# Packed attention and a gated feed-forward on one core: another order of the first batch's loads, and twelve products ahead of TensorE's order

## The chip, the core and the metric

The kernel runs on one core of a Trainium2 chip. TensorE (PE in the rows) multiplies matrices and transposes through a product with an identity matrix, VectorE (DVE), ScalarE (ACT) and GpSimd (POOL) work on elements, and SyncE (SP) issues transfers between the chip's memory and the core's own. ScalarE can issue transfers too. The metric is the time of one execution in microseconds (us), from the first to the last instruction of the core with the little that lies around it. Of the kernel before there are three timed runs, 739.72 to 740.54 us, median 739.77 us.

## The reference

```python
# batch 8, heads H = 8, seq S = 576, D = 64; p has 32 rows for each head
def sm_attn(qq, kk, vv):
    s = scale * np.matmul(qq, kk.transpose(0, 1, 3, 2))
    s = s - np.max(s, axis=-1, keepdims=True)
    a = np.exp(s)
    a = a / (np.sum(a, axis=-1, keepdims=True) + 1e-09)
    return np.matmul(a, vv)

p_packed = sm_attn(p, k, v)              # stage 1: 32 queries for each head
out = sm_attn(q, p_packed, p_packed)     # stage 2: 576 queries on 32 keys
x = out.transpose(0, 2, 1, 3).reshape(4608, 512)
result = (x @ w_a) * (x @ w_b) @ w_out   # w_a, w_b: 512 x 1536, w_out: 1536 x 512
```

All inputs and the output are float32.

## The kernel before

The kernel goes through the batch in eight steps of 576 tokens. For each it computes stage 1 of the attention (`stage1`, two groups of four heads), stage 2 (`stage2`, the same two groups) and then the feed-forward. The feed-forward has a trick: instead of forming x and multiplying it by w_a and w_b, `g_tiles` (L332) multiplies the 32 packed rows of each head with w_a and w_b first, and `mm1` (L351) multiplies the attention weights of stage 2 with that. The product of the two halves goes through `mm2_part` (L377) with w_out. The large operands are split in a high and a low part (`a_hi`, `a_lo`, `ghi`, `glo`), and three products make up one.

While TensorE does the feed-forward of one batch step, the attention of the next is woven in between its products. Only the first batch step has nothing to be woven into: its inputs have to be loaded, turned and sent through both attention stages before the first product of `mm1` can run. This stretch at the start is what the change touches.

The inputs of the first batch step are loaded by `load_first` (k and q, in three parts each: 0 and 1 are 512 rows of four heads each, 2 is the rest of all heads), `load_v` (two groups) and `load_p`. `turn_first` (L147, L152) turns k and q on TensorE, into a bank of PSUM, and VectorE (L149) or ScalarE (L149, L154) copies the result to `xT`. `turned` (L236) does so for p, and later for the result of stage 1 (`ppT`, L237). Stage 1's first products are L247, its softmax L253 to L261, its turned weights L271 to L274, its second products L281. Stage 2's first products are L297, and its softmax runs on VectorE, ScalarE and GpSimd, L302 to L319.

The weights w_a, w_b and w_out are stored as float32 words that have to be changed before use, in three steps per piece, which the orders call A (`high_word`, L189, ScalarE), B (`low_word`, L197 on ScalarE or L194 on VectorE or GpSimd) and C (`both_words`, L200, VectorE). Twelve buffers hold pieces (512 KB each); C frees one, and with it the next load can go.

Every engine does its instructions in the order in which they are written (`manual_schedule`), so four strings of names set the work of each engine: `FIRST` is the order of the first loads, `START` that of all steps up to the first `mm1`, `PLAN_0` and `PLAN` what is woven into the first batch step's feed-forward and the later ones'. In `FIRST` a name is an input and a part (p0, k0, k1, k2, q0 to q2, v0, v1; w1 loads one piece of a weight). In `START`, T turns p, k and q turn a part, S and r are the steps of stage 1, P turns its result, s are the steps of stage 2, A, B and C convert a piece, L loads for the next batch step, and g starts `g_tiles`. W is `warm` (L519): nine products of the identity with a tile of k, which nobody reads (L524, 128x512 each).

```python
    FIRST = ("p0 k0 k2 k1 q0 v0 q1 v1 q2 w1 w1 w1 w1 w1 w1 w1 w1 w1 w1 w1")
    START = ("T0 k0 k4 k1 k3 k2 q0 S0 S1 r0 r1 q1 r1 r0 r0 r1 r0 q2 r1 q3 q4 P0 s0 B s1 W A s0 B A A s0 s0 B s1 C "
```

Of the kernel before, what the change touches and what calls it, by code (L numbers as in the profile page):

```python
# [19 lines left out]
def tile_packed_attn_gated_ffn(  # L20
# [20 lines left out]
    nc = tc.nc  # L41
    B, H, S, D = q.shape
# [3 lines left out]
    P = 128  # L46
    R, E = 4, 2
# [6 lines left out]
    TR = HS - 2 * P  # L54
# [17 lines left out]
    ident = const.tile([P, P], F32, name="ident")  # L72
# [18 lines left out]
    def bank_pair(s=False):  # L91
        return ps_s.tile([P, 2, 512], F32, name="s") if s else ps_m.tile([P, 2, 512], F32, name="m")
# [9 lines left out]
    def load(src, key, b, i):  # L102


        t = ld.tile([P, R, XH, TL], F32, name=f"nat{i}")
        rows = src[b, R * i:R * i + R].rearrange("h s d -> (h s) d")
        rows = rows.rearrange("(y l u) d -> u l y d" if key == "k" else "(y u l) d -> u l y d", u=2, l=TL)
        for u in range(2):
            for w in range(2):
                g = 64 * u + 32 * w  # L110
                nc.sync.dma_start(
                    out=t[g:g + TL].rearrange("l h x d -> l (h x) d"), in_=rows[u][:, :, TL * w:TL * w + TL])
        nats[key, b, i] = t

    def turn(key, b, i):

        t = nats.pop((key, b, i))
        xT = ld.tile([P, R, HS], F32, name=f"xT{i}")
        nc.vector.transpose(out=xT.rearrange("p h t -> p (h t)"), in_=t.rearrange("p h x d -> p (h x d)"))  # L119
        xTs.setdefault((b, key), []).append(xT)  # L120
# [2 lines left out]

    firsts = {}

    def load_first(src, key, part):

        if part < 2:
            t = scratch.tile([P, R, 4 * D], F32, name=f"{key}n{part}")
            nc.sync.dma_start(  # L130
                out=t, in_=src[0, R * part:R * part + R, 0:4 * P, :].rearrange("h (p i) d -> p h (i d)", i=4))
        else:
            t = scratch.tile([P, H, 2 * D], F32, name=f"{key}n{part}")
            nc.sync.dma_start(out=t[0:TR], in_=src[0, :, 4 * P:S, :].rearrange("h (p u) d -> p h (u d)", u=2))
        firsts[key, part] = t

    def turn_first(key, n):
# [17 lines left out]

    vts, p_nat = {}, {}

    def load_v(b, e):


        t = ld.tile([P, R, NT, D], F32, name="vt") if b or e == 0 else scratch.tile([P, R, NT, D], F32, name="vt1")
        vv = v[b].rearrange("(r e) s d -> e s r d", e=E)[e]
        n = 2 if b else 4
        for i in range(4 // n):
            nc.sync.dma_start(
                out=t[:, :, n * i:n * i + n, :].rearrange("p r u d -> p r (u d)"),
                in_=vv[n * P * i:n * P * i + n * P].rearrange("(p u) r d -> p r u d", u=n).rearrange("p r u d -> p r (u d)"))
        for u in range(2):
            nc.sync.dma_start(
                out=t[TR * u:TR * u + TR, :, 4, :],  # L170
                in_=vv[4 * P:S].rearrange("(p u) r d -> u p r d", u=2)[u])
        vts[b, e] = t

    def load_p(b):
        t = sm.tile([P, E + 1, D], F32, name="p_nat", bufs=1)
        for e in range(E + 1):
            nc.sync.dma_start(out=t[:, e, :], in_=p[b].rearrange("(r e) j d -> e r j d", e=E)[e % E])  # L177
        p_nat[b] = t

    def xT_cols(b, key, u, h, cols=slice(0, HS)):  # L180
# [50 lines left out]
    def turned(dst, src, back=0):  # L231

        tp = bank()
        cols = src.rearrange("p e d -> p (e d)")
        for i in range(2):
            nc.tensor.transpose(tp[:, P * i:P * i + P], cols[:, 64 * (i ^ back):64 * (i ^ back) + P], ident)  # L236
        nc.vector.tensor_copy(out=dst.rearrange("p i r j -> p (i r j)"), in_=tp[:, 0:2 * P])  # L237
# [178 lines left out]
    def drain(g):  # L416
        for _ in g:
            pass

    def emit(b, plan, tasks={}):  # L420

        for name in plan.split():
            if name in tasks:
                next(tasks[name], None)
                continue
            if name == "W":
                warm()
                continue
            if name in "ABCD":
                convert(name)  # L430
                continue
            what, e = name[:-1], int(name[-1])
            n = b + (e // 2 if b or what[0] == "L" else 0)
            if n >= B:
                continue
            if what == "S":
                if e == 0:
                    st[b] = [stage1(b, 0), stage1(b, 1), stage2(b, 0), stage2(b, 1)]
                next(st[b][e])
            elif what == "s":  # L440
                next(st[b][2 + e], None)
            elif what == "r":
                next(st[b][e], None)
            elif what == "T":
                turned(pT, p_nat.pop(n))
            elif what == "P":
                turned(ppT[:, b % 2:b % 2 + 2], pp.pop(b), b % 2)
            elif what in ("k", "q"):
                turn(what, n, e % 2) if b else turn_first(what, e)
            elif what == "Lk":  # L450
                load(k, "k", n, e % 2)
            elif what == "Lq":
                load(q, "q", n, e % 2)
            elif what == "Lv":
                load_v(n, e % 2)
            elif what == "Lp":
                load_p(n)

    st = {}

    FIRST = ("p0 k0 k2 k1 q0 v0 q1 v1 q2 w1 w1 w1 w1 w1 w1 w1 w1 w1 w1 w1")
    START = ("T0 k0 k4 k1 k3 k2 q0 S0 S1 r0 r1 q1 r1 r0 r0 r1 r0 q2 r1 q3 q4 P0 s0 B s1 W A s0 B A A s0 s0 B s1 C "
             "A s1 B s0 C s1 A s1 C B B Lp2 C A B A s0 s1 B C B B s0 B g A C A A s1 Lv2 Lk2 C C A A C B B Lk3 C s1")
    WAYS = ("000000022220202120012012011200010010")
    TURN = ("0001110101")
    SUBS = ("0100")
# [1 line left out]
    PLAN = (" | S0 | r0 |  | r0 | r0 |  | r0 Lv1 |  | S1 | r1 | q0 Lk2 | r1 |  |  | r1 q1 Lk3 |  | r1 Lv2 |  |  | "  # L468
            "T2 P0 |  |  | s0 s0 s1 g s0 |  | s1 | Lp4 s0 s1 s1 k2 | s0 | s0 | s1 s0 | s1 Lq2 | s1 | k3 Lq3")
    PLAN = dict(enumerate(PLAN.split("|")))  # L470
    PLAN_0 = ("A | C C | B A B A | B C C B C | A A | C | B | C B A T0 k0 Lp2 A | A A B B C Lq0 | C C k1 | A B A | "
# [3 lines left out]
    PLAN_0 = dict(enumerate(PLAN_0.split("|")))  # L475

# [13 lines left out]
    def convert(x):  # L490

        if x == "D":
            if wo_f32:
                split_wout(wo_f32.pop(0))
                load_pieces(2)
            return
        if not to_do[x]:
            return
        c, n = to_do[x].pop(0)
        if (c, n) not in raws:  # L500
            load_pieces(1)
        raw = raws[c, n]
        if x == "A":
            high_word(raw)
        elif x == "B":
            low_word(raw, int(WAYS[pieces.index((c, n))]))
        else:
            assert len(to_do["A"]) <= len(to_do[x]) and len(to_do["B"]) <= len(to_do[x])
            if c < NC:
                i, rr = divmod(n, 2)  # L510
                both_words(w_ab[:, c, 2 * rr:2 * rr + 2, 2 * P * i:2 * P * i + 2 * P], raw)
            else:
                t = sm.tile([P, DO], F32, name="wo_f32", bufs=1)
                both_words(t, raw)
                wo_f32.append(t)
            del raws[c, n]
            load_pieces(2)

    def warm(n=9):  # L519

        x = bank_pair()[:, 0, :]
        t = firsts["k", 0].rearrange("p h t -> p (h t)")
        for _ in range(n):
            nc.tensor.matmul(out=x, lhsT=ident, rhs=t[:, 0:512], start=True, stop=True)  # L524

    def next_g(b):

        gnext[:] = g_tiles(b, 0)
        yield

    ET = mybir.EngineType
    ep(tc.manual_schedule(engines={ET.PE, ET.DVE, ET.Activation, ET.Pool, ET.SP}))
    for name in FIRST.split():
        what, i = name[0], int(name[1])
        if what == "p":
            load_p(0)
        elif what == "v":
            load_v(0, i)
        elif what == "w":
            load_pieces(i)  # L540
        else:
            load_first(k if what == "k" else q, what, i)
    gnext = []
    tasks = {"g": next_g(0)}
    emit(0, START, tasks)
    drain(tasks["g"])
    early.__exit__(None, None, None)
# [5 lines left out]
    for b in range(B):  # L553
        plan = dict(PLAN if b else PLAN_0)
        slot, tasks = [0], {"g": next_g(b + 1)}
# [73 lines left out]
```

## Time and profile before

| | us |
|---|---|
| median of three timed runs | 739.77 |
| the profiled execution, its own time | 739.7 |
| its span, first to last instruction | 737.9 |
| TensorE busy | 724.8 (98%) |
| first transfer of k issued | 2.74 |
| first transpose of k on TensorE | 7.29 |
| first product of stage 1 | 12.92 |
| first product of mm1 | 35.09 |

Times inside the profile are counted from the start of the span. The profiled execution's own time is 1.8 us longer than its span; that part lies around the span. A row of an engine's timeline gives start, length, engine, line, the written and read tiles, shapes and the number of instructions merged into it; ends of products are modelled, so the distance from one start to the next tells more than the length. In brackets stands how long the engine was idle before, and what ended that. TensorE's 98% leave some 13 us of the span in which no product is recorded, and nearly all of those lie before the first product of `mm1`.

### The profile page before, as it was taken

What the parts mean: (1) busy time and instruction counts of PE and PEld (TensorE: products, weight loads), DVE (VectorE), ACT (ScalarE), POOL (GpSimd) and SP (SyncE); (2) the same over time, 40 slices, a digit from 0 to 9 for tenths busy, and PEclk for the clock granted to TensorE, in tenths of its full rate; (3) what the DMA queues carried; (4) which work ended last, traced back from release to release, by engine and by line L of the source; (5) the groups of instructions that cost most, each with busy time, mean ns of one, the idle gap of its engine ahead of it and who ended that gap; (6) DMA issues with size and microseconds to landing.
All of it is one profiled execution on the core that took longest, in us unless ns stands there. A gap on an engine that the chain in (4) does not pass through costs nothing.

```text
span 737.9 us, 13756 instructions
## 1 busy us (share of the span) xinstructions
PE 724.8 (98%) x5862; PEld 606.0 (82%) x5862; DVE 302.4 (41%) x487; ACT 282.6 (38%) x495; POOL 212.5 (29%) x154
## 2 busy tenths in 40 slices
PE   6899999999999999999999999999999999999998
PEld 4488977888888888888888888888888888888887
DVE  2888655456114561344503545045610456023200
ACT  3788744553125531444204442144311543134300
POOL 0586752334003340234202341033400334023300
PEclk9999999999999999999999999999999999999999
DMA  8999945250501514033310333115050100000001
GB/s 251 379 260 297 257 88 99 57 97 17 97 30 33 98 30 84 16 66 70 74 48 16 65 71 77 47 33 97 5 104 30 34 1 17 28 15 2 1 29 43
DMA packets 171005, 58.30 MB, mean 79 GB/s; under 512 B 140608, under 2 KB 158784, under 8 KB 170944
## 3 DMA queue, kind: packets, MB, share of 16 engines
q1 hardware_dynamic: 170944, 57.43, 31.9%
q8 instruction: 46, 0.75, 0.4%
q14 instruction: 15, 0.12, 0.1%
HBM read 47.97 MB, written 9.44 MB: 78 GB/s over the span
## 4 chain that ended last, share of the span: by engine, by line
PE 95%; DVE 2%; DMA 1%; ACT 1%; issue 0%; SPq 0%; DVEq 0%; ACTq 0%
PE m L351 42%; PE m L377 40%; PE x L332 6%; PE s L281 2%; PE s L247 1%; PE s L271 1%; PE s L297 1%; DMA raw<-in_moe_w_b_dram 1%; DMA kn<-in_k_dram 1%; PE x L236 0%; DVE w_ab L200 0%; PE x L147 0%; PE m L297 0%; PE m L147 0%; SPq L177 0%
## 5 line engine op out<-in xcount | busy, mean ns | idle before, releaser
L377 PE MATMUL m<-wo,h_hi 128*128 128x512 f32 (+1 forms) x888 | 268.7, 385 | 0.0
L86 POOL TENSOR_TENSOR h_lo<-asb,h_hi 128x576 fp32r<-128x576 f32 x96 | 139.1, 1449 | 411.5 <-ACT h_hi L370 411.2
L377 PEld LDWEIGHTS m<-wo,h_hi 128*128 128x128 f32 x888 | 164.2, 188 | 39.0 <-DVE t L302 5.0
L366 DVE TENSOR_TENSOR asb<-m,asb 128x576 f32<-128x576 f32 x96 | 72.7, 757 | 281.9 <-PE m L351 278.6
L351 PE MATMUL m<-a_hi,ghi 128*128 128x288 f32 x768 | 170.7, 304 | 1.6 <-ACT ghi L338 1.5
L377 PE MATMUL m<-wo,h_lo 128*128 128x512 f32 (+1 forms) x444 | 170.4, 384 | 0.0
L351 PE MATMUL m<-a_lo,ghi 128*128 128x288 f32 x768 | 164.0, 295 | 0.3 <-DVE a_lo L86 0.3
L351 PEld LDWEIGHTS m<-a_hi,ghi 128*128 128x128 f32 x768 | 122.2, 188 | 37.5 <-issue 15.9
L351 PE MATMUL m<-a_hi,glo 128*128 128x288 f32 x768 | 133.5, 295 | 0.0
L351 PEld LDWEIGHTS m<-a_lo,ghi 128*128 128x128 f32 x768 | 123.5, 188 | 0.5 <-DVE a_lo L86 0.5
L370 ACT CAST h_hi<-asb 128x576 fp32r<-128x576 f32 x96 | 64.7, 674 | 143.6 <-DVE asb L366 143.5
L351 PEld LDWEIGHTS m<-a_hi,glo 128*128 128x128 f32 x768 | 112.8, 188 | 0.2 <-DVE glo L86 0.2
L377 PEld LDWEIGHTS m<-wo,h_lo 128*128 128x128 f32 x444 | 83.4, 188 | 16.6
L86 DVE TENSOR_TENSOR glo<-x,ghi 128x512 fp32r<-128x512 f32 x96 | 61.8, 686 | 53.3 <-ACT ghi L338 53.3
L363 ACT COPY asb<-m 128x576 f32<-128x576 f32 x96 | 61.6, 641 | 36.7 <-PE m L351 29.0
L412 ACT COPY asb<-m 128x512 f32<-128x512 f32 x24 | 14.1, 587 | 134.8 <-PE m L377 133.6
L332 PE MATMUL x<-w_ab,ppT 64*32 64x512 f32 x768 | 55.4, 597 | 0.2 <-DVE w_ab L200 0.2
L338 ACT CAST ghi<-x 128x512 fp32r<-128x512 f32 x96 | 51.4, 588 | 5.9 <-PE x L332 5.9
L119 DVE STREAM_TRANSPOSE xT<-nat 128x1152 f32<-128x1152 f32 x28 | 38.3, 1368 | 0.0
L412 ACT COPY wo_f<-m 128x512 f32<-128x512 f32 x11 | 6.5, 588 | 55.2 <-PE m L377 55.2
L315 POOL TENSOR_TENSOR t<-t,sum 128x576 f32<-128x576 f32 x14 | 16.5, 1178 | 25.0 <-DVE sum L314 25.0
L189 ACT ACTIVATE raw<-raw 128x512 f32<-128x512 f32 x36 | 23.1, 683 | 0.1
(108 smaller groups left out, 408.1 us busy)
## 6 DMA issues: line engine op xcount, KB each, us to landing
nat<-in_k_dram SPq DMA_DIRECT2D x56, 144.0 KB
nat<-in_q_dram SPq DMA_DIRECT2D x56, 144.0 KB
vt<-in_v_dram SPq DMA_DIRECT2D x28, 256.0 KB
raw<-in_moe_w_a_dram SPq DMA_DIRECT2D x12, 512.0 KB
raw<-in_moe_w_b_dram SPq DMA_DIRECT2D x12, 512.0 KB
raw<-in_moe_w_out_dram SPq DMA_DIRECT2D x12, 512.0 KB
out_dram<-asb SPq DMA_DIRECT2D x17, 256.0 KB
out_dram<-wo_f SPq DMA_DIRECT2D x10, 256.0 KB
```

The lines of the kernel that those rows point to most:

```text
L86: return eng.tensor_tensor(out=dst, in0=src, in1=hi.bitcast(F32), op=ALU.subtract)
L119: nc.vector.transpose(out=xT.rearrange("p h t -> p (h t)"), in_=t.rearrange("p h x d -> p (h x d)"))
L189: nc.scalar.activation(out=high, in_=high, func=AF.Prelu, scale=2.0 ** -112, alpha=-2.0 ** 32)
L315: eng.tensor_tensor(out=s2, in0=s2, in1=sum2.unsqueeze(2).broadcast_to([P, TU, J]), op=ALU.mult)
L332: nc.tensor.matmul(out=gps[e][J * r:J * r + J, :], lhsT=ppT[rows, 2 * (b % 2), r, :], rhs=w_ab[rows, c, r, :], start=True, stop=True)
L338: nc.scalar.copy(out=ghi[:, e], in_=gps[e])
L351: nc.tensor.matmul(out=ps[:, half, 0:HS], lhsT=gt[:, kt, i, :], rhs=at[:, kt, HS * half:HS * half + HS], start=(n == 0 and kt == 0), stop= ...
L363: nc.scalar.copy(out=asb, in_=pa[:, :, 0:HS])
L366: nc.vector.tensor_tensor(out=asb, in0=pb[:, :, 0:HS], in1=asb, op=ALU.mult)
L370: nc.scalar.copy(out=hh, in_=flat)
L377: nc.tensor.matmul(out=o[:, cols], lhsT=ht[:, c0:c0 + P], rhs=wt[:, cols], start=(ft == 0 and n == 0), stop=(ft == NFT - 1 and n == 2))
L412: nc.scalar.copy(out=ob, in_=o)
```

## The change

Four things are changed, all for the first batch step.

- The order of the first loads. k's first part is issued first, p and the first group of v (written P0 and V0) are issued by ScalarE instead of SyncE, q's second part moves ahead of v, and the first piece of the weights ahead of q's last part.
- V12: twelve products of the identity with itself (128x128 each) at the head of TensorE's order, which nobody reads.
- W8 instead of W: eight instead of nine of the large ones.
- In `START` and `PLAN_0` some conversion steps (A, B, C), one L and one q stand elsewhere by a few places.

```diff
-    def load_first(src, key, part):
+    def load_first(src, key, part, eng):
...
-            nc.sync.dma_start(
+            eng.dma_start(
...
-    def load_v(b, e):
+    def load_v(b, e, eng=nc.sync):
...
-    def load_p(b):
+    def load_p(b, eng=nc.sync):
...
-            if name == "W":
-                warm()
+            if name[0] in "VW":
+                warm(ident if name[0] == "V" else firsts["k", 0].rearrange("p h t -> p (h t)")[:, 0:512], int(name[1:]))
...
-    FIRST = ("p0 k0 k2 k1 q0 v0 q1 v1 q2 w1 w1 w1 w1 w1 w1 w1 w1 w1 w1 w1")
-    START = ("T0 k0 k4 k1 k3 k2 q0 S0 S1 r0 r1 q1 r1 r0 r0 r1 r0 q2 r1 q3 q4 P0 s0 B s1 W A s0 B A A s0 s0 B s1 C "
...
+    FIRST = ("k0 P0 k2 k1 q0 q1 v1 V0 w1 q2 w1 w1 w1 w1 w1 w1 w1 w1 w1 w1")
+    START = ("V12 T0 k0 k4 k1 k3 k2 q0 S0 S1 r0 r1 q1 r1 r0 r0 r1 r0 q2 r1 q3 q4 P0 s0 B s1 W8 A B s0 A B A s0 s0 "
...
-    def warm(n=9):
-
-        x = bank_pair()[:, 0, :]
-        t = firsts["k", 0].rearrange("p h t -> p (h t)")
+    def warm(t, n):
+
+        x = bank_pair()[:, 0, 0:t.shape[1]]
         for _ in range(n):
-            nc.tensor.matmul(out=x, lhsT=ident, rhs=t[:, 0:512], start=True, stop=True)
+            nc.tensor.matmul(out=x, lhsT=ident, rhs=t, start=True, stop=True)
...
-        what, i = name[0], int(name[1])
+        what, i = name[0].lower(), int(name[1])
+        eng = nc.scalar if name[0].isupper() else nc.sync
```

The head of TensorE's order before, up to the first products of stage 1 (p_nat is p as loaded, kn and qn the parts of k and q):

```order
L236 MATMUL x<-ident,p_nat 128x128 x2
L147 MATMUL x<-ident,kn_101 128x128 x4
L152 MATMUL x<-ident,kn_103 128x32 x8
L147 MATMUL x<-ident,kn_101 128x128 x4
L147 MATMUL m<-ident,kn_105 128x128 x8
L147 MATMUL x<-ident,qn_107 128x128 x4
L247 MATMUL s<-xT_147,pT 32x288 x2
```

The same place in the changed program:

```order
L524 MATMUL m<-ident 128x128 x12
L236 MATMUL x<-ident,p_nat 128x128 x2
L147 MATMUL x<-ident,kn_97 128x128 x4
L152 MATMUL x<-ident,kn_103 128x32 x8
L147 MATMUL x<-ident,kn_97 128x128 x4
L147 MATMUL m<-ident,kn_105 128x128 x8
L147 MATMUL x<-ident,qn_107 128x128 x4
L247 MATMUL s<-xT_160,pT 32x288 x2
```

The twelve products are new, and the turn of p still stands ahead of all turns of k; the rest keeps its order.

SyncE's transfers before, from the start (raw is a piece of the weights):

```order
L177 DMA p_nat<-in_p_dram 128x1x64 x3
L130 DMA kn_101<-in_k_dram 128x4x256
L134 DMA kn_103<-in_k_dram 32x8x128
L130 DMA kn_105<-in_k_dram 128x4x256
L130 DMA qn_107<-in_q_dram 128x4x256
L165 DMA vt<-in_v_dram 128x4x256
L169 DMA vt<-in_v_dram 32x4x64 x2
L130 DMA qn_113<-in_q_dram 128x4x256
L165 DMA vt_115<-in_v_dram 128x4x256
L169 DMA vt_115<-in_v_dram 32x4x64 x2
L134 DMA qn_119<-in_q_dram 32x8x128
L210 DMA raw<-in_moe_w_a_dram 128x2x512 x2
```

SyncE's transfers now:

```order
L130 DMA kn_97<-in_k_dram 128x4x256
L134 DMA kn_103<-in_k_dram 32x8x128
L130 DMA kn_105<-in_k_dram 128x4x256
L130 DMA qn_107<-in_q_dram 128x4x256
L130 DMA qn_109<-in_q_dram 128x4x256
L165 DMA vt_111<-in_v_dram 128x4x256
L169 DMA vt_111<-in_v_dram 32x4x64 x2
L210 DMA raw<-in_moe_w_a_dram 128x2x512
L134 DMA qn_121<-in_q_dram 32x8x128
```

The head of ScalarE's order now; before, it began with the table load in the fourth of these rows:

```order
L177 DMA p_nat<-in_p_dram 128x1x64 x3
L165 DMA vt<-in_v_dram 128x4x256
L169 DMA vt<-in_v_dram 32x4x64 x2
L154 ACT_TABLE_LOAD
L154 COPY xT_160<-x 128x4x32
L154 COPY xT_161<-x 128x4x32
L149 COPY xT_161<-m 128x2x256
L149 COPY xT_197<-x 128x2x256
```

Six transfers left SyncE's order and stand ahead of everything that ScalarE does. Of the six, the last two carry a wait for an earlier transfer: the first of them for k's first part, the second for one of p's.

## Rows read from the trace of the kernel before

**Rows 1.** The page's first part (busy time, share of the span, instructions) for TensorE, and the first line of its chain of work that ended last (share of the span by engine).

```profile
PE 724.8 (98%) x5862; PEld 606.0 (82%) x5862; DVE 302.4 (41%) x487; ACT 282.6 (38%) x495; POOL 212.5 (29%) x154
...
PE 95%; DVE 2%; DMA 1%; ACT 1%; issue 0%; SPq 0%; DVEq 0%; ACTq 0%
```

**Rows 2.** The waits of TensorE from 36 us to the end, all of them: line, what it waited for, us in total, times, longest.

```profile
PE m L351 <- DVE a_lo L86: 0.3, 1, 0.3
```

**Rows 3.** The chain of work that ended last, its first pieces in order of time: start us, us, what.

```profile
0.74 0.74 SPq L177
...
2.16 0.53 SPq L177
...
2.74 4.50 DMA kn<-in_k_dram
...
7.29 1.11 PE x L147 x4
```

**Rows 4.** TensorE's timeline: start us, us, engine, line, operation, tiles, shapes, count, and idle time before.

```profile
4.23 0.89 PE L236 MATMUL x<-ident,p_nat 128*128 128x128 f32 x2 [4.23 <-DMA p_nat<-in_p_dram]
...
10.23 1.91 PE L147 MATMUL m<-ident,kn 128*128 128x128 f32 x8
11.93 1.06 PE L147 MATMUL x<-ident,qn 128*128 128x128 f32 x4
12.92 1.00 PE L247 MATMUL s<-xT,pT 64*32 64x288 f32 x24
...
18.42 0.66 PE L147 MATMUL m<-ident,qn 128*128 128x128 f32 x4
19.01 0.90 PE L281 MATMUL x<-vt,a1T 128*32 128x64 f32 x40
...
20.43 0.68 PE L152 MATMUL x<-ident,qn 32*128 32x32 f32 x8
21.04 0.44 PE L236 MATMUL x<-ident,pp 128*128 128x128 f32 x2
...
23.90 7.99 PE L524 MATMUL m<-kn,ident 128*128 128x512 f32 x18
32.04 1.57 PE L332 MATMUL x<-w_ab,ppT 64*32 64x512 f32 x16 [0.15 <-DVE w_ab L200]
35.09 0.54 PE L351 MATMUL m<-a_hi,ghi 128*128 128x288 f32 x2 [1.48 <-ACT ghi L338]
```

**Rows 5.** SyncE's issuing of transfers, the same columns.

```profile
4.85 0.51 SPq L165 DMA_DIRECT2D vt<-in_v_dram  x1
5.40 1.49 SPq L169 DMA_DIRECT2D vt<-in_v_dram  x2
...
12.32 0.90 SPq L210 DMA_DIRECT2D raw<-in_moe_w_a_dram  x2
```

**Rows 6.** Transfers issued in the first 24 us, by tile: count, KB each.

```profile
kn<-in_k_dram SPq DMA_DIRECT2D x2, 512.0 KB
qn<-in_q_dram SPq DMA_DIRECT2D x2, 512.0 KB
vt<-in_v_dram SPq DMA_DIRECT2D x2, 512.0 KB
kn<-in_k_dram SPq DMA_DIRECT2D x1, 128.0 KB
...
p_nat<-in_p_dram SPq DMA_DIRECT2D x3, 32.0 KB
```

**Rows 7.** Stretches of time: length, busy time and instructions of each engine, granted clock of TensorE (1.00 is full), share of the transfer engines that is busy, GB/s.

```profile
5.00:10.00 5.00, 2.83 (x16) 2.32 (x16) 1.12 (x2) 0.43 (x2) 0.00 (x0) 1.00 1.09 335
...
15.00:20.00 5.00, 4.16 (x98) 2.90 (x96) 2.52 (x11) 3.63 (x9) 0.00 (x0) 1.00 1.08 337
...
25.00:30.00 5.00, 5.00 (x13) 2.14 (x12) 4.84 (x10) 4.26 (x8) 2.11 (x2) 1.00 1.05 387
30.00:35.00 5.00, 3.46 (x21) 0.91 (x19) 4.96 (x8) 3.85 (x8) 4.81 (x3) 1.00 1.06 388
```

**Rows 8.** The timelines of GpSimd (one row: the identity is made) and ScalarE, columns as in rows 4.

```profile
1.01 0.29 POOL masks.py:199 TENSOR_SCALAR_AFFINE_SELECT ident<-ident 128x128 f32<-128x128 f32 x1
...
0.73 1.28 ACT L154 ACT_TABLE_LOAD   x1 [0.73 <-PEq L613]
9.43 0.43 ACT L154 COPY xT<-x 128x128 f32<-128x128 f32 x2 [7.41 <-PE x L152]
11.32 0.59 ACT L149 COPY xT<-m 128x512 f32<-128x512 f32 x1 [1.47 <-PE m L147]
...
25.74 0.69 ACT L309 ACTIVATE s<-s 128x576 f32<-128x576 f32 x1 [1.26 <-POOL s L307]
26.33 0.66 ACT L197 ACTIVATE raw<-raw 128x512 uint32<-128x512 uint32 x1
```

**Rows 9.** The chain of work that ended last where the weights come into it, columns as in rows 3.

```profile
34.26 5.21 DMA raw<-in_moe_w_b_dram
...
39.83 1.15 DVE w_ab L200
...
43.92 3.46 PE m L351 x24
```

**Rows 10.** The longest of SyncE's waits up to 60 us, columns as in rows 2.

```profile
SPq L210 <- DVE w_ab L200: 6.9, 4, 2.5
```

More of the change, by code (lines that the diff above doesn't have):

```diff
@@ L133, in load_first @@
             t = scratch.tile([P, H, 2 * D], F32, name=f"{key}n{part}")
-            nc.sync.dma_start(out=t[0:TR], in_=src[0, :, 4 * P:S, :].rearrange("h (p u) d -> p h (u d)", u=2))
+            eng.dma_start(out=t[0:TR], in_=src[0, :, 4 * P:S, :].rearrange("h (p u) d -> p h (u d)", u=2))
         firsts[key, part] = t
@@ L164, in load_v @@
         for i in range(4 // n):
-            nc.sync.dma_start(
+            eng.dma_start(
                 out=t[:, :, n * i:n * i + n, :].rearrange("p r u d -> p r (u d)"),
@@ L168, in load_v @@
         for u in range(2):
-            nc.sync.dma_start(
+            eng.dma_start(
                 out=t[TR * u:TR * u + TR, :, 4, :],
@@ L172, in load_v @@
         vts[b, e] = t
-    def load_p(b):
+    def load_p(b, eng=nc.sync):
         t = sm.tile([P, E + 1, D], F32, name="p_nat", bufs=1)
         for e in range(E + 1):
-            nc.sync.dma_start(out=t[:, e, :], in_=p[b].rearrange("(r e) j d -> e r j d", e=E)[e % E])
+            eng.dma_start(out=t[:, e, :], in_=p[b].rearrange("(r e) j d -> e r j d", e=E)[e % E])
         p_nat[b] = t
@@ L459, in tile_packed_attn_gated_ffn @@
     st = {}
-    FIRST = ("p0 k0 k2 k1 q0 v0 q1 v1 q2 w1 w1 w1 w1 w1 w1 w1 w1 w1 w1 w1")
-    START = ("T0 k0 k4 k1 k3 k2 q0 S0 S1 r0 r1 q1 r1 r0 r0 r1 r0 q2 r1 q3 q4 P0 s0 B s1 W A s0 B A A s0 s0 B s1 C "
-             "A s1 B s0 C s1 A s1 C B B Lp2 C A B A s0 s1 B C B B s0 B g A C A A s1 Lv2 Lk2 C C A A C B B Lk3 C s1")
+    FIRST = ("k0 P0 k2 k1 q0 q1 v1 V0 w1 q2 w1 w1 w1 w1 w1 w1 w1 w1 w1 w1")
+    START = ("V12 T0 k0 k4 k1 k3 k2 q0 S0 S1 r0 r1 q1 r1 r0 r0 r1 r0 q2 r1 q3 q4 P0 s0 B s1 W8 A B s0 A B A s0 s0 "
+             "B s1 C A s1 s1 s0 C s1 A C B B Lp2 C A B A s0 s1 B C s0 B g A B C A A s1 Lv2 B Lk2 C C A A C B B Lk3 "
+             "C s1")
     WAYS = ("000000022220202120012012011200010010")
@@ L470, in tile_packed_attn_gated_ffn @@
     PLAN = dict(enumerate(PLAN.split("|")))
-    PLAN_0 = ("A | C C | B A B A | B C C B C | A A | C | B | C B A T0 k0 Lp2 A | A A B B C Lq0 | C C k1 | A B A | "
[2 rows of a table removed]
+    PLAN_0 = ("A | C C | B A B A | B C C B C | A A | C | B | B C A T0 k0 Lp2 B A | A A B C Lq0 | C k1 | A B A | S0 "
[2 rows of a table added]
               "A B | s1 s0 | Lv2 | D | s0 s1 s0 | k2 s0 s1 C k3 | s1 |  | Lq2 D s0 s1 s1 Lq3 s1")
@@ L533, in tile_packed_attn_gated_ffn @@
     for name in FIRST.split():
-        what, i = name[0], int(name[1])
+        what, i = name[0].lower(), int(name[1])
+        eng = nc.scalar if name[0].isupper() else nc.sync
         if what == "p":
-            load_p(0)
+            load_p(0, eng)
         elif what == "v":
-            load_v(0, i)
+            load_v(0, i, eng)
         elif what == "w":
@@ L541, in tile_packed_attn_gated_ffn @@
         else:
-            load_first(k if what == "k" else q, what, i)
+            load_first(k if what == "k" else q, what, i, eng)
     gnext = []
```

4 rows, old and new, of the table PLAN_0 are left out of this document.

## The prediction, made before the changed kernel was run

> **What bounds the kernel now.** I read the page's busy shares first: TensorE is busy for 98% of the span and makes up 95% of the chain that ended last [rows 1]. The reader is to see that little is to be had anywhere but where TensorE waits. The waits by engine, asked from 36 us to the end, hold one of 0.3 us and no other [rows 2]. So from the first products of the feed-forward, at 35.09 us, the kernel runs as fast as TensorE does, and a change of the start is worth what it brings these products forward. Then I read the chain from the front. It goes through p's three issues on SyncE, k's first transfer from 2.74 to 7.24 us, and the transposes of k on TensorE from 7.29 us [rows 3]. TensorE's timeline continues it: stage 1 starts at 12.92 us, the first mm1 at 35.09 us [rows 4]. From about 23 us the chain sits on VectorE, which is busy 4.84 and 4.96 of each 5 us between 25 and 35 us [rows 7], and the weights touch it once, with a load issued at 34.26 us that takes 5.21 us [rows 9]. So there are three clocks to move: k and q arriving, TensorE turning them, and the weights arriving.
>
> **k's arrival.** k's first part takes p's place in SyncE's order, so its issue goes from 2.74 to 0.74 us [rows 3], 2.0 us earlier. It took 4.50 us from issue to landing; from 0.74 us this gives 5.24 us. p now travels beside it: three transfers of 32 KB [rows 6], 98 KB at 335 GB/s [rows 7] are 0.3 us more, so 5.5 us.
>
> **q's arrival.** Stage 1 stands behind the first turn of q in TensorE's order, so what it needs is k whole and q's first part. Behind k's first 512 KB are 128, 512 and 512 KB [rows 6], 1.18 MB, at 335 to 350 GB/s 3.4 us: 8.9 us if nothing comes between. But v's first 512 KB, which stood behind q in the same order, are now issued by ScalarE. Its three issues of p take what SyncE's took, until 2.7 us [rows 3], and v's takes 0.51 us [rows 5], so v is under way before most of k. The trace has transfers of one issuing engine only and doesn't show how two share. The bounds: v behind q, 8.9 us; v wholly ahead of q, 1.5 us more, 10.4 us. I take 10.4 us, because the transfer engines are full in this stretch (share 1.09 [rows 7]): what v takes early, q gets late. As a test, the old order gives by the same rates 7.24 + 3.4 = 10.6 us for q and 1.5 us more, 12.1 us, for v; the first load of the weights, which waits for v, was issued at 12.32 us [rows 5].
>
> The Trainium skill, DMA: Bandwidth & Descriptors, section "Issuing engines are not separate DMA queues", speaks against this part of the change: transfers run on the same 16 engines and interleave, whichever engine started them, and a second issuing engine only saves the time of issuing. By it q lands near 10.4 us, and the two issuing engines bring no more bytes; without it, near 8.9 us. The trace has one queue and shows neither.
>
> **TensorE's part.** The twelve products need only the identity, ready at 1.30 us [rows 8]. A large product is two instructions (18 for nine [rows 4]), so these are 24. What one takes I bound by transposes of the same 128 columns. Eight take 10.23 to 11.93 us, 0.21 us each; later four take 18.42 to 19.01 us, 0.15 us each [rows 4]. So 24 end between 1.3 + 24 x 0.15 = 4.9 us and 1.3 + 24 x 0.21 = 6.4 us. The same two paces bound what follows: p's turn is 0.3 to 0.4 us (two transposes), and from the first turn of k to stage 1 it took 12.92 - 7.29 = 5.63 us; at the later pace 20 transposes of 0.15 us and eight small ones of 0.61 us together (20.43 to 21.04 us) are 3.6 us. The profile's granted clock reads 1.00, the upper level of 2.4 GHz, in the stretches on both sides of the step [rows 7], yet the same instruction is 1.4 times as long in one. Before the step TensorE had worked without a gap from 7.29 us, and before that it had mostly waited for transfers.
>
> The Trainium skill, TensorE: Matmul & The Clock Gate, section "What's actually happening", says that the idle array is throttled and that activity releases it. The durations agree, the granted clock in the rows does not. By it the twelve products would be what releases the clock; it also says that the moment is not tied to the kernel's start and differs from run to run, which speaks against counting on it.
>
> I take the long pace for the twelve products and the short one for all behind them: 6.4 + 0.3 + 3.6 = 10.3 us for the start of stage 1 if TensorE alone decided. With q at 10.4 us, four turns more (0.6 us) end at 11.0 us. The later of the two decides: 11.0 us instead of 12.92 us, **1.9 us earlier**. All long: 6.4 + 0.4 + 5.63 = 12.5 us, 0.4 us earlier. With q at 8.9 us TensorE's 10.3 us decides, 2.6 us earlier.
>
> **ScalarE's six issues.** They stand ahead of its table load. p and v's first are issued by 3.2 us, the fifth waits for k's first part (5.5 us), and two such issues took 1.49 us [rows 5], so they end at 7.0 us and the table load of 1.28 us [rows 8] at 8.3 us. Queued behind it is the copy of k's small part, with TensorE's turn of q behind that. Before it ran at 9.43 us and the next copy at 11.32 us [rows 8]; now the first runs by 8.3 us and the next after k's second part, near 9.5 us. Cost nothing, covered by q's arrival; were that cover gone (q at 8.9 us), the copies would end at 8.3 + 0.4 + 0.6 = 9.3 us and stage 1 would still wait for TensorE.
>
> **Weights.** The same bytes pass ahead of them, through engines that are full from 5 us on (335 to 388 GB/s [rows 7]), and start 2.0 us earlier, less p's 0.3 us that now share the time: 1.7 us. The load at 34.26 us belongs to a kind that waits for a buffer freed by VectorE's conversions [rows 9, 10], so its issue moves with VectorE, and only its 5.21 us depend on what is queued. I count 1.9 us for it, and 1.7 us as its lower bound.
>
> **The rest.** W8 takes 8 x 0.89 = 7.1 us instead of 8.0 us. Before, W ended at 31.89 us and g_tiles still waited 0.15 us for VectorE [rows 4]; both move, so nothing is gained. The conversion that moves ahead of the first exp fills 1.26 us in which ScalarE waited for GpSimd [rows 8] and takes 0.66 us: no cost, and no gain while VectorE is full. The moved steps of PLAN_0 lie where TensorE waits for nothing [rows 2]: nothing to gain, and I allow 0.5 us of loss for a conversion that comes late.
>
> **The sum.** 739.7 us of the profiled execution (737.9 us of span and 1.8 us around it, which I leave) less 1.9 us is 737.8 us. The median of the runs shown, 739.77 us, is the same within 0.1 us.
>
> **Rivals.** First, v's transfer does not hold up q, and TensorE decides: 2.6 us earlier, 737.1 us; with the twelve products at the short pace too, 4.9 us, p's turn waits for its data near 5.5 us, and 5.5 + 0.3 + 3.6 = 9.4 us comes near q's 8.9 + 0.6 us, so 3.4 us earlier, 736.3 us. For it speaks that SyncE issued q soon after k; against it the full engines. Second, the gain is mostly hidden: TensorE stays at the long pace until stage 1 (0.4 us, 739.3 us), or the weights hardly come forward, and the load that landed at 39.47 us holds the chain up to the mm1 at 43.92 us [rows 9] where it was: about 0.7 us, 739.0 us. For it speaks that the rows don't show what raised the pace; against it that TensorE, which before was mostly idle ahead of k, is now at work there. Third, slower: p is late. p's turn is ahead of k's in TensorE's order, and p's packets now share the engines with k. With the long pace behind it, stage 1 starts 0.4 + 5.6 = 6.0 us after p's turn begins, so it is later than before if p lands after 6.9 us (after 9.0 us at the short pace). If p came through with q only, 8.9 us, stage 1 would start at 14.9 us, 2.0 us later: 741.7 us. Against it: p had landed at 4.23 us, 1.5 us after its last issue [rows 3, 4].
>
> **How the numbers follow.** The forecast case has 0.56, its own range 1.4 to 2.6 us: 737.1 to 738.3 us. The first rival has 0.14, the second 0.24, the third 0.06. The range that holds eight in ten takes in most of the first rival and of the second: 736.2 to 739.2 us. A change of 0.2%, 1.5 us, is about what a measurement of this kernel can tell from none, so faster means under 738.3 us: nearly all of the forecast case and all of the first rival, 0.66. The second rival and the forecast's edge give 0.28 for the same, the third rival 0.06 for slower.
>
> **What will show it.** In the changed trace k's first turn should begin near 6.7 us, at the short pace (0.6 instead of 1.04 us for four), stage 1 near 11 us with a wait for q in front of its turn, the first mm1 near 33.2 us, and no wait of TensorE after that. If the turn of q doesn't wait, the first rival holds; if the transposes of k still take 0.21 us, the second; if p's turn waits past 7 us, the third. The forecast is wrong if stage 1 moves and the first mm1 doesn't, which would put the bound in the weights.

## The result, and the profile after

The changed kernel took 743.96 us (median of 5 runs, 743.55 to 744.23) against 739.77 us before: a ratio of 1.0053, 95% interval 1.0039 to 1.0066. It is 4.2 us slower; the forecast was 737.8 us and its range ended at 739.2 us. The profiled execution took 743.96 us with a span of 742.2 us, 4.3 us more than before.

The waits of TensorE over the whole span, largest first (line, what it waited for, us in total, times, longest), in the changed kernel:

```profile
PE x L236 <- DMA p_nat<-in_p_dram: 3.5, 2, 1.7
PE x L332 <- DVE w_ab L200: 1.7, 1, 1.7
PE m L351 <- ACT ghi L338: 1.5, 1, 1.5
PE m L524 <- POOL ident masks.py:199: 1.4, 1, 1.4
```

TensorE now waits longest for p, whose turn stands first in its order. The other three are one wait each, at the start or up to the first mm1; behind that no wait is over 0.3 us, as in [rows 2]. So the loss is made in the first 40 us. The chain that ended last begins with p as well, where before it began with k [rows 3]:

```profile
0.74 1.15 ACTq L177
...
2.50 8.06 DMA p_nat<-in_p_dram
...
10.60 0.38 PE x L236
```

A load of 32 KB that ScalarE issued at 2.5 us took 8.06 us. Before, the same load, the third of p, was issued by SyncE at 2.16 us [rows 3], and p's turn began at 4.23 us [rows 4]. TensorE's timeline of the changed kernel, to be laid beside [rows 4]:

```profile
1.36 5.49 PE L524 MATMUL m<-ident 128*128 128x128 f32 x24 [1.36 <-POOL ident masks.py:199]
8.56 0.30 PE L236 MATMUL x<-ident,p_nat 128*128 128x128 f32 x1 [1.71 <-DMA p_nat<-in_p_dram]
10.60 0.38 PE L236 MATMUL x<-ident,p_nat 128*128 128x128 f32 x1 [1.74 <-DMA p_nat<-in_p_dram]
10.78 1.06 PE L147 MATMUL x<-ident,kn 128*128 128x128 f32 x4
...
13.66 1.91 PE L147 MATMUL m<-ident,kn 128*128 128x128 f32 x8
...
16.36 1.20 PE L247 MATMUL s<-xT,pT 64*32 64x288 f32 x22
...
38.91 0.53 PE L351 MATMUL m<-a_hi,ghi 128*128 128x288 f32 x2 [1.47 <-ACT ghi L338]
```

The twelve products end at 6.85 us. Then there is one transpose of p at 8.56 and one at 10.60 us; in between TensorE does nothing. The transposes of k follow with no wait, but at the long pace (1.06 us for four, 1.91 us for eight). Before, k's turns took as long (1.11 and 1.91 us [rows 4]), and from the first of them to stage 1 it was 5.63 us, now 5.58 us: up to stage 1 the loss against the kernel before is the wait for p alone. Stage 1 starts 3.44 us later than before, the first mm1 3.82 us later, the whole span 4.3 us. The windows show two more things (length, busy time of each engine, granted clock, share of the transfer engines, GB/s):

```profile
8.00:10.00 2.00, 0.30 (x1) 0.14 (x1) 0.00 (x0) 1.20 (x1) 0.00 (x0) 1.00 1.12 336
10.00:12.00 2.00, 1.40 (x7) 1.07 (x8) 0.55 (x2) 0.08 (x1) 0.00 (x0) 0.69 1.10 328
12.00:14.00 2.00, 2.00 (x14) 1.94 (x14) 0.66 (x2) 0.43 (x2) 0.00 (x0) 0.50 0.78 212
14.00:16.00 2.00, 2.00 (x11) 2.00 (x10) 0.98 (x2) 0.59 (x1) 0.00 (x0) 0.50 0.73 156
```

After the idle time the granted clock falls to 0.50, its lower level of 1.2 GHz, just while k is turned. Before, the column read 1.00 [rows 7] while the same turns took as long; the last section comes back to this. And from 12 to 16 us the transfer engines are no longer full: 212 and 156 GB/s. SyncE's issues, and the longest of its waits up to 20 us, say why:

```profile
2.27 3.54 SPq L130 DMA_DIRECT2D qn<-in_q_dram  x2
6.47 0.37 SPq L165 DMA_DIRECT2D vt<-in_v_dram  x1
10.58 0.81 SPq L169 DMA_DIRECT2D vt<-in_v_dram  x2
13.68 0.38 SPq L210 DMA_DIRECT2D raw<-in_moe_w_a_dram  x1
...
SPq L169 <- DMA p_nat<-in_p_dram: 3.7, 1, 3.7
```

Between 6.84 and 10.58 us SyncE issued nothing. It stood for 3.7 us in front of a small load of v, waiting for a load of p: the program gives the transfers of both issuing engines their completion semaphores from one rotation (the trace names eight in this stretch), and this issue takes over one that p's load still holds. The first load of the weights went out at 13.68 us instead of 12.32 us [rows 5].

### The profile page after: what moved, and what is told of

It reads as the page before. It is cut to its first block, busy times and chain, and to the rows that moved or that the text cites. A ratio compares the mean times of both kernels' runs of the same rounds, so it can differ in the third digit from the quotient of the medians.

```text
span 742.2 us, 13800 instructions
## 1 busy us (share of the span) xinstructions
PE 728.8 (98%) x5884; PEld 610.9 (82%) x5884; DVE 302.4 (41%) x487; ACT 282.6 (38%) x495; POOL 212.2 (29%) x154
## 4 chain that ended last, share of the span: by engine, by line
PE 93%; DMA 2%; DVE 2%; ACT 1%; issue 0%; ACTq 0%; POOL 0%; SPq 0%; DVEq 0%; POOLq 0%
PE m L351 40%; PE m L377 40%; PE x L332 6%; PE s L281 2%; PE s L247 1%; DMA p_nat<-in_p_dram 1%; PE s L297 1%; PE s L271 1%; DMA vt<-in_v_dram 1%; DMA raw<-in_moe_w_out_dram 1%; PE x L236 1%; PE m L297 0%; PE m L147 0%; PE x L147 0%; ACT ghi L338 0%
```

## The experiments

What is to be told apart is why p is late and what its lateness costs. Theory A: p is late because it is alone in ScalarE's queue and takes turns there with SyncE's large transfers. Its rival, theory B: v's 512 KB, which ScalarE now issues early, take the bandwidth. Further questions are what the twelve products, ScalarE's six issues and the new order do. The diffs are against the changed kernel unless said otherwise; in the list of first loads a small letter is issued by SyncE, a capital by ScalarE. No kernel leaves out work that the output needs. Each was timed beside the kernel before, whose medians were 739.74 us beside the first four runs, 740.10 us beside the next four and 740.14 us beside the last four; each ratio is to its own.

**p back in SyncE's queue, v's first part still in ScalarE's.**

```
-    FIRST = ("k0 P0 k2 k1 q0 q1 v1 V0 ...
+    FIRST = ("p0 k0 k2 k1 q0 q1 v1 V0 ...
```

> The changed kernel, but p's three loads go through SyncE's queue at its head again, as before (k's first part fourth); v's first group stays with ScalarE and the twelve products stay. Theory A (p's loads, alone in ScalarE's queue, are held up by k's and q's in SyncE's, and TensorE's turn of p stands ahead of k's turns): p lands near 4.2 us again, TensorE goes from the twelve products (end near 6.9 us) into p's and k's turns with no wait over 1 us, k's turns at 0.15 us each, stage 1 starts near 11 to 12 us instead of 16.36 us, and the time is 738 to 740.5 us. Theory B (v's load through ScalarE's queue, or the new order of the steps, costs the time): stage 1 starts later than before's 12.92 us and the time stays above 742 us.

740.94 us (740.19 to 742.21), ratio 1.0015 [1.0006, 1.0024]. Three of the 4.2 us are gone, so p's queue is the main cause; what is left is v's. Its TensorE timeline:

```profile
6.36 0.33 PE L236 MATMUL x<-ident,p_nat 128*128 128x128 f32 x1 [0.48 <-DMA p_nat<-in_p_dram]
8.94 0.66 PE L147 MATMUL x<-ident,kn 128*128 128x128 f32 x4 [2.25 <-DMA kn<-in_k_dram]
...
11.28 1.97 PE L147 MATMUL m<-ident,kn 128*128 128x128 f32 x8 [0.24 <-DMA kn<-in_k_dram]
...
14.03 0.95 PE L247 MATMUL s<-xT,pT 64*32 64x288 f32 x24
```

p is turned by 6.7 us, but k's first part comes at 8.9 us, where before it had landed at 7.24 us [rows 3]: v's 512 KB, alone in ScalarE's queue from 0.73 us, take their share first (up to 5 us ScalarE's queue moves 0.58 MB, SyncE's 0.09 MB). Neither theory's number fits whole; A is the larger part, B a smaller one, and it acts on k.

**p's turn moved behind k's.**

```
-    START = ("V12 T0 k0 k4 k1 k3 k2 q0 S0 ...
+    START = ("V12 k0 k4 k1 k3 k2 T0 q0 S0 ...
```

> The changed kernel with one step moved: TensorE turns p after k's five turns instead of ahead of them; the loads are as in the changed kernel. Theory A: p still lands near 10.6 us, but k's turns run from 6.9 us on, most of them at the short pace, and stage 1 starts right behind p's and q's turns, near 11.7 us; time 738 to 740 us. Theory C (q and the rest of k land as late as p, so the whole queue is slow): k's turns wait too, stage 1 starts after 14 us, time 741.5 us or more.

741.38 us, widely scattered (738.71 to 745.84), ratio 1.003 [1.0013, 1.0048]. TensorE and ScalarE:

```profile
5.65 0.60 PE L147 MATMUL x<-ident,kn 128*128 128x128 f32 x4
...
8.00 1.09 PE L147 MATMUL m<-ident,kn 128*128 128x128 f32 x8 [0.23 <-DMA kn<-in_k_dram]
11.30 0.65 PE L236 MATMUL x<-ident,p_nat 128*128 128x128 f32 x2 [2.21 <-ACT xT L154]
...
12.73 1.20 PE L247 MATMUL s<-xT,pT 64*32 64x288 f32 x22
```

```profile
5.80 3.69 ACTq L169 DMA_DIRECT2D vt<-in_v_dram  x2
9.52 1.28 ACT L154 ACT_TABLE_LOAD   x1 [9.52 <-DMA p_nat<-in_p_dram]
10.81 0.43 ACT L154 COPY xT<-x 128x128 f32<-128x128 f32 x2
```

k is there by 5.65 us and is turned at the short pace. Then TensorE waits 2.21 us for ScalarE's copy, which stands behind ScalarE's own issues: two small loads of v wait until 9.49 us for p's semaphores, and the table load follows. So stage 1 comes only 0.19 us earlier than before. The six issues on ScalarE cost nothing only as long as p is later still. Why the median is 1.6 us above the kernel before is not shown: the profiled execution (740.42 us) has its first mm1 at 35.43 us, 0.34 us later than before. The two fastest runs, 738.71 and 739.09 us, have a mean granted clock of 1.000, the three slowest, 743.70 to 745.84 us, one of 0.993 to 0.995.

**v back in SyncE's queue, p alone in ScalarE's.**

```
-    FIRST = ("k0 P0 k2 k1 q0 q1 v1 V0 ...
+    FIRST = ("k0 P0 k2 k1 q0 q1 v1 v0 ...
```

> The changed kernel, but v's first group goes through SyncE's queue too, so that p's three loads are all that ScalarE issues. Theory A in the form that p's loads take turns with whole loads of SyncE's queue: v stands behind p in ScalarE's queue and can't hold it up, p's third load lands near 10 us as before, time 743 to 744.5 us. Theory B (v's 512 KB in ScalarE's queue are what delays p): p lands by 6 us and the time is under 740 us.

744.25 us (743.64 to 744.55), ratio 1.0061 [1.0049, 1.0073]: as slow as the change. p's two transposes begin at 8.79 and 11.46 us, stage 1 at 16.90 us. p is late with no v in its queue, so theory B falls for p.

**The twelve products taken out.** (`V12` taken from the head of the order.)

> The changed kernel without the twelve products at the head of TensorE's order. Theory A: TensorE waits for p until 10.6 us anyhow, k's turns run at the long pace (0.21 us) in both, so the time stays within 0.7 us of the changed kernel's 743.96 us. Theory D (the products themselves cost the time, by keeping TensorE from p's turn or by the clock that fell after them to a granted 0.5): the time falls by more than 1.5 us.

743.91 us (742.99 to 744.11), ratio 1.0054 [1.0041, 1.0066]: no difference from the change. p's transposes begin at 8.44 and 10.96 us, k's run at the long pace, stage 1 starts at 16.81 us. The products lie wholly in time in which TensorE waits, and what they do for the pace is lost in the wait behind them.

**All first loads by SyncE, k's first part ahead of p.**

```
-    FIRST = ("k0 P0 k2 k1 q0 q1 v1 V0 w1 ...
+    FIRST = ("k0 p0 k2 k1 q0 q1 v0 v1 w1 ...
```

> The changed kernel with every first load on SyncE's queue: k's first part, then p's three loads, then the rest of k, q, v. The twelve products and the new order stay. Theory A (p was held up only because it stood alone in another queue): p lands right behind k's first part, by 6.5 us, k's turns begin by 7 us at the short pace, stage 1 starts between 10.5 and 11.5 us, and the time is 737 to 738.5 us, faster than before by 0.2% or more. Theory C (k, q and p land late together, whatever the queue): stage 1 starts after 12.9 us and the time is 740 us or more.

739.08 us (738.44 to 742.95, eight of twelve runs below 739.3), ratio 0.9997 [0.9984, 1.001]. TensorE:

```profile
6.44 0.60 PE L147 MATMUL x<-ident,kn 128*128 128x128 f32 x4
...
9.93 0.63 PE L147 MATMUL x<-ident,qn 128*128 128x128 f32 x4 [0.48 <-DMA qn<-in_q_dram]
10.49 0.69 PE L247 MATMUL s<-xT,pT 64*32 64x288 f32 x20
...
18.82 0.65 PE L152 MATMUL x<-ident,qn 32*128 32x32 f32 x8 [1.06 <-DMA qn<-in_q_dram]
...
33.88 0.53 PE L351 MATMUL m<-a_hi,ghi 128*128 128x288 f32 x2 [1.47 <-ACT ghi L338]
```

The same transfers through one queue undo the whole loss: p is there by 5.95 us, and stage 1 starts at 10.49 us. Of these 2.4 us, 1.2 us are left at the first mm1 (q's last part, issued behind a load of weights, comes 1.06 us late). Nothing is left at 84.9 us: the transpose L272 there begins at 84.92 us, and at 84.82 us before. The profiled execution was one of the four slower ones (739.91 us), so this holds for it, and not for the median. The chain in between runs through a load of weights and the ScalarE work behind it:

```profile
56.38 7.97 DMA raw<-in_moe_w_b_dram
...
64.37 0.69 ACT raw L189
...
67.89 1.85 PE m L351 x12
```

**The kernel before, with the twelve products alone.**

```
-    START = ("T0 k0 ...
+    START = ("V T0 k0 ...
...
+            if name == "V":
+                x = bank_pair()[:, 0, 0:P]
+                for _ in range(12):
+                    nc.tensor.matmul(out=x, lhsT=ident, rhs=ident, start=True, stop=True)
+                continue
```

> The kernel before with the twelve products at the head of TensorE's order and nothing else. If they raise TensorE's pace in time for k and p holds nothing up: p's turn at 5.7 to 7 us, k's turns from 7.3 us at the short pace until they wait for k's second part near 9.5 us, stage 1 near 11.7 us because q lands near 10.6 us; time 738.3 to 739.2 us. If the pace falls again while TensorE waits, or the products come too late: 739.5 us or more.

741.16 us (738.8 to 744.58), ratio 1.0011 [0.9995, 1.0027]: no gain can be told. p's turn starts at 5.83 us behind the products, then TensorE waits 2.13 us for k; the granted clock reads 0.83 from 5 to 10 us and 0.50 from 10 to 15 us, and stage 1 starts at 13.98 us, later than the 12.92 us without products. That is k's landing and not the products: k's first turn begins 1.05 us later in this execution (8.34 against 7.29 us), and from there to stage 1 it takes 5.64 us, as before (5.63 us).

**The new order alone**: the old list of first loads and no twelve products, with the changed kernel's steps and eight large products.

> The kernel before with the new order of the steps (START and PLAN_0 of the changed kernel, eight large products instead of nine) but the old loads and no twelve products. The prediction's term for this is nothing, at most 0.5 us of loss: 739.7 to 740.3 us. Theory B (the new order costs the time): over 741 us.

740.16 us (739.31 to 744.13), ratio 1.0008 [0.9996, 1.002]; stage 1 at 12.78 us, the first mm1 at 34.82 us. With the old start, the order makes no difference that can be told.

**p's third load replaced by a copy on VectorE.**

```
-        for e in range(E + 1):
+        for e in range(E + 1 if b else E):
             eng.dma_start(out=t[:, e, :], in_=p[b].rearrange("(r e) j d -> e r j d", e=E)[e % E])
+        if b == 0:
+            nc.vector.tensor_copy(out=t[:, E, :], in_=t[:, 0, :])
```

> The changed kernel, but of p's three loads the third, a repetition of the first, is replaced by a copy on VectorE in SBUF, so ScalarE issues two loads of p. Theory A in the form that each load of p waits for its turn behind whole loads of k and q: p is complete near 8.5 us, when its second load landed, instead of 10.6 us, stage 1 starts near 14 us, and the time is 741 to 742.3 us. If p's packets only move slowly as a whole (by bytes), two thirds of them land only a third sooner or not at all, 743 us or more.

741.26 us (740.59 to 742.63), ratio 1.0017 [1.0008, 1.0025]. p's turn starts at 8.66 us, both transposes together, and stage 1 at 14.70 us. One load of 32 KB fewer brings p 1.94 us forward and the time 2.7 us. By its bytes the load is 0.1 us.

**k's first part as four transfers of 128 KB.**

```
-            eng.dma_start(out=t, in_=src[0, R * part:R * part + R, 0:4 * P, :] ...
+            hs = [slice(h, h + 1) for h in range(R)] if key == "k" and part == 0 else [slice(0, R)]
+            for h in hs:
+                eng.dma_start(out=t[:, h], in_=src[0, R * part + h.start:R * part + h.stop, 0:4 * P, :] ...
```

> The changed kernel, but k's first part (512 KB) is loaded by four transfers of 128 KB, one for each head, on SyncE's queue; p stays alone with v's first group on ScalarE's. Theory A1 (the two queues take turns transfer by transfer, so each of p's loads waits behind one whole transfer of the other queue): with small transfers ahead p's turns come sooner, p is complete by 7 us, stage 1 starts by 13 us, and the time is 741 us or less. Theory A2 (ScalarE's queue is served late or slowly whatever the size of the other's transfers): p is complete after 8.5 us and the time stays above 742.5 us.

739.94 us (739.06 to 741.14), ratio 0.9993 [0.9982, 1.0004]. p's transposes begin at 6.80 and 7.57 us, k's at 7.73 us at the short pace, stage 1 at 12.86 us. So p can come in time through ScalarE's queue when less stands beside it. The whole gain isn't the smaller transfers', though, because SyncE's list ran on more slowly too:

```profile
0.74 1.88 SPq L132 DMA_DIRECT2D kn<-in_k_dram  x4
2.93 0.38 SPq L137 DMA_DIRECT2D kn<-in_k_dram  x1
3.92 0.39 SPq L132 DMA_DIRECT2D kn<-in_k_dram  x1
7.54 0.93 SPq L132 DMA_DIRECT2D qn<-in_q_dram  x2
```

q's two transfers waited for semaphores of the rotation and went out at 7.54 us, when p had landed; the smaller transfers and the missing q both left less in p's way. For p's first load the two can be told apart, since q had no part in its wait. The profile counts the packets of each queue (q1 carries SyncE's transfers, q10 ScalarE's; count, MB, share of the 16 transfer engines; here one row of a transfer is a packet). The changed kernel in three stretches, 0 to 4, 4 to 4.75 and 4.75 to 6.75 us, and behind the dots this run, 0 to 2.37 and 2.37 to 3.33 us:

```profile
q1 hardware_dynamic: 463, 0.47, 41.1%
q1 hardware_dynamic: 330, 0.21, 97.4%
q10 hardware_dynamic: 132, 0.03, 19.5%
q1 hardware_dynamic: 572, 0.54, 112.3%
...
q1 hardware_dynamic: 122, 0.12, 16.8%
q1 hardware_dynamic: 233, 0.21, 67.0%
q10 hardware_dynamic: 131, 0.03, 15.1%
```

In the changed kernel ScalarE's queue moves nothing until 0.47 MB of k are through, most of its first part, then one load of p, then nothing for 2 us more, while 0.54 MB of SyncE's pass and the next loads of p, issued by 3.1 us, wait. With k in four transfers p's first load moves behind 0.12 MB, about one of the four. So the first wait follows the size of the transfer in front, and is no fixed time or number of bytes.

**All by SyncE, with q's last part ahead of v.**

```
-    FIRST = ("k0 P0 k2 k1 q0 q1 v1 V0 w1 q2 w1 ...
+    FIRST = ("k0 p0 k2 k1 q0 q1 q2 v0 v1 w1 w1 ...
```

> All first loads on SyncE's queue, k's first part, then p, then k, all of q, v, and the weights last; twelve products and the new order as in the changed kernel. In the run with all loads on SyncE TensorE waited 1.1 us for q's last part, which stood behind the first weights. If that wait was lost time: it goes, the first mm1 moves from 33.9 to near 32.8 us, and the time falls to 737.5 to 738.5 us. If the weights set the end of this stage: the first mm1 moves, TensorE waits for converted weights between 40 and 70 us instead, and the time stays at 738.8 to 739.5 us.

739.07 us, scattered (737.88 to 744.24), ratio 0.9993 [0.9976, 1.0009]. Stage 1 starts at 10.57 us, the first mm1 at 33.09 us, 2.0 us earlier than before; at 83.8 us 1.0 us of it is left, and the profiled span is 736.9 us, 1.0 us shorter. The mm1 product that starts at 43.92 us before comes 1.84 us earlier here, the one at 60.17 us only 0.97 us. What took the other half is the next batch's k, which lies between, here in the chain of waits:

```profile
53.65 3.27 DMA nat<-in_k_dram
...
57.11 1.39 DVE xT L119
...
58.54 0.71 PE s L247 x16
```

**The same without the twelve products.**

> The run before without the twelve products. If they are worth what the prediction gave them, k's turns go back to the long pace: from p's turn at about 5.8 us stage 1 starts near 11.9 us instead of 10.5 us, and the time is 0.5 to 1.5 us longer than with them. If the weights set the end anyway, the two are within 0.4 us.

739.36 us (738.67 to 740.73), ratio 0.999 [0.9982, 0.9998]: the only version whose interval lies below 1, by 0.8 us; as one of thirteen versions that is weak evidence of a gain. k is turned at the long pace, stage 1 starts at 12.39 us, the first mm1 at 34.56 us. The products bring stage 1 1.8 us forward (10.57 us), but the median only 0.3 us, and the runs with them spread over 6.4 us instead of 2.1.

**q's last part ahead of v, with the order of the kernel before** (its steps and its nine large products, with the twelve products kept at the head).

> The same loads and twelve products, but START and PLAN_0 as in the kernel before (nine large products). The prediction's term for the new order is nothing: within 0.5 us of the run with the new order. If the new order is what makes the weights late in the run with all loads on SyncE, this one is faster by 0.7 us or more.

742.76 us (739.94 to 744.26), ratio 1.0031 [1.002, 1.0043]. The start is as early as with the new order (stage 1 10.70 us, first mm1 33.58 us), but the time is 3.7 us longer. TensorE:

```profile
61.37 0.97 PE L247 MATMUL s<-xT,pT 64*32 64x288 f32 x20 [2.58 <-DVE xT L119]
...
62.91 0.68 PE L351 MATMUL m<-a_lo,ghi 128*128 128x288 f32 x2
...
65.23 0.43 PE L351 MATMUL m<-a_hi,ghi 128*128 128x288 f32 x2
```

With the old order the last load of the next batch's k goes out at 55.57 us instead of 53.65 us, TensorE waits 2.58 us for it, and after this wait the granted clock is 0.67 from 60 to 65 us: a pair of products takes 0.68 us instead of 0.43 us. The old order fits the old start; brought forward, it runs into the next batch's loads. Two of the twelve runs escape: at a mean granted clock of 1.000 they took 739.94 and 740.39 us, the other ten, at 0.995 to 0.998, 742.46 to 744.26 us.

## Why the prediction was wrong

**The bound** was read rightly for a loss: the 3.8 us at the first mm1 are 4.3 us at the end, and TensorE waits for little behind it. For a gain it was not, as the part on the weights shows.

**k's arrival: the step that failed.** k's first part was forecast at 5.5 us and is there by 5.65 us (p's turn moved behind). But p was charged 0.3 us, its 98 KB at the full rate, as if transfers of two queues shared by bytes. Its last load came at 10.6 us. By then SyncE's queue had moved 1.97 MB, which is all of k (1.18 MB), q's first part (0.52 MB) and some of its second: p came through about when q's first part did. Rival 3 had this mechanism, its condition (p after 6.9 us) and its place, and the 6.0 us that it put between p's turn and stage 1 were 5.76 us (10.60 to 16.36 us, from the last of p's two transposes). It had p at 8.9 us where it was 10.6 us, so 2.0 us where 4.2 us were lost, and a chance of 0.06, because p had been quick in its old place. That argument was no evidence: in the old place p stood first in the only queue.

The three p loads were each held up for about as long as one large transfer of the other queue takes: the two waits end 2.04 us apart, one load fewer is 1.94 us, and 512 KB at 335 GB/s are 1.6 us. The packet counts show one queue standing still while the other moves 0.47 and 0.54 MB. Whether a turn is exactly one transfer can't be told from them, since they add up all 16 transfer engines. And with p alone in ScalarE's queue the third load did not stand still but trickled, 129 packets from 8.2 to 10.75 us beside 832 of SyncE's. What decides between standing and trickling no run here shows. The Trainium skill, DMA: Bandwidth & Descriptors, section "Queues, rings and completion order", says that each transfer engine goes round the queues that have work and drains a whole packet, of several descriptors, from one before it takes the next. That the queues take turns agrees with the counts; how long the page's packet is can't be read from them, since they count rows and not groups of rows. The section that the prediction cited, "Issuing engines are not separate DMA queues", was right in that no bytes came faster (336 GB/s from 8 to 10 us), but gives no order among the loads, and the order was what mattered.

**q's arrival** was no limit in the changed kernel. With all loads on SyncE q's first turn waited until 9.93 us, inside the bounds of 8.9 to 10.4 us. What v's place costs fell elsewhere: with p fixed, v in ScalarE's queue held up k, 8.9 us (first run), which no term had.

**TensorE's part** holds where nothing waits. The products end at 6.85 us (forecast 6.4; 5.71 to 6.85 us in the other runs that have them). With p in time k's first turn began at 6.44 us at the short pace (0.60 us for four, as forecast), and stage 1 at 10.49 us against 11.0 us. In the changed kernel TensorE stood still for 3.45 us of the 3.75 us between 6.85 and 10.60 us, and the granted clock fell to 0.50. So of the 5.4 us by which stage 1 missed the forecast (16.36 against 11.0), 4.2 us are p's turn (10.6 against 6.4). The other 1.2 us are the pace: from p's turn to stage 1 it took 5.76 us where the forecast had 3.9 us at the short pace, and 0.7 us of that difference the forecast had filled with a wait for q.

**ScalarE's six issues** at nothing: right only behind the late p. The estimate that they end at 7.0 us had the fifth issue wait for k's first part and gave the sixth no wait of its own. By the semaphores in the trace's rows the fifth waited for p's first load (it went out at 5.81 us) and the sixth for p's second (8.45 us); they ended at 8.8 us, and at 9.5 us in the run with p's turn moved, where TensorE waited 2.21 us for them. The same rotation stopped SyncE for 3.7 us, which the prediction didn't see: it looked for what stands behind a wait on ScalarE alone.

**Weights** would have failed even with p in time. They were to come 1.7 to 1.9 us forward. In the changed kernel they went back 1.36 us (issue at 13.68 us). Where the start did come 2.4 us forward, the gain was gone at 85 us behind a load of weights; with q's last part ahead, half of 2.0 us was left. So the second rival's thought, that the loads hold the end where it was, was true of the start that the forecast described. Even with p in time the forecast of 1.9 us would have been about 1 us too good.

**The order** at nothing (0.5 us at most): right with the old start (1.0008 [0.9996, 1.002]), wrong with the early one, where the old order loses 3.7 us. The price of an order was read from a trace in which the rest stood still.

Still open: what sets the length of a queue's turn; and how much of the scatter of the versions with the twelve products (6.4 against 2.1 us) is TensorE's clock. With q's last part ahead, the runs without products all have a mean granted clock of 1.000, and of those with them the six fastest 1.000 but for one, the six slowest 0.997 to 0.999. With all loads on SyncE the two don't go together: 738.79 us at 0.995, 741.66 us at 1.000. No run varies the clock alone.

## What to carry over

A small load that something waits for early belongs near the head of the queue that carries the large ones (p behind one 512 KB load was there by 5.95 us), not alone in a second queue: there its few bytes didn't protect it, and each of three loads was held up anew. Before moving issues to another engine, follow their completion semaphores as well, since an issue that takes over a busy one stops everything behind it on its engine, computation too. And a start brought forward is worth only what the next late transfer leaves of it: price it at the first loads of the next stage, not at the first product.

## What was not expected of the hardware

Products that only keep TensorE busy bought a shorter start when real work followed at once (stage 1 at 10.57 us with them, 12.39 us without), and nothing when a wait followed: in the kernel before with the products alone, TensorE waited 2.13 us, then ran at a granted clock of 0.50, and took 5.64 us from k's first turn to stage 1, as long as without them (5.63 us). Of the Trainium skill, TensorE: Matmul & The Clock Gate, section "What's actually happening", the runs show both directions: activity raises the clock, and idleness lowers it again.

The column of the granted clock doesn't show the slow start: in the changed kernel without the products it reads 1.00 from 10 to 18 us while four transposes of k take 1.06 us, just as they do in the changed kernel at 0.50. Only the durations of equal instructions tell it. The reason lies in the record: the trace's list of clock levels begins with a rise, at 16.94 us in that run and at 13.58 us in the kernel before, and ahead of its first entry the column reads 1.00. In the kernel before four equal transposes take 1.06 us at 11.93 us and 0.66 us at 14.57 us, on either side of that rise. So the granted clock and the durations, which the prediction found at odds, agree where there is a record.
